# A tuned attention-then-gMLP kernel: more numerator buffers, weights loaded earlier, a shared start, a tail with its own bank waits

## The chip, the cores and the metric

The kernel runs on one core of one Trainium2 chip. The metric is the device time of that core in microseconds (us). Kernels that are compared run on the same chip, in turns with the kernel before. A run over 1.5% above the fastest of its kernel in the same rounds counts as slow.

## The reference, cut to what matters

```python
# q, k, v: (8 batches, 8 heads, 576 rows, 64)
scores = scale * np.matmul(q, k.transpose(0, 1, 3, 2))
thresh = np.max(scores, axis=-1, keepdims=True) - tau
scores = np.where(scores >= thresh, scores, -1000000000.0)
attn = np.exp(scores - max);  attn = attn / (sum + 1e-09)     # shortened
x = (attn @ v) as (batch, 576, 512)                           # shortened
# gMLP:
h = np.maximum(x @ w_in, 0.0);  u, v = halves of h
v_n = normalised v
v_s = np.einsum('ts,bsd->btd', w_spatial, v_n) + b_spatial[None, :, None]
out = (u * v_s) @ w_out
```

## The kernel before

Two heads make a pair, and there are 32 pairs. A pair has four tiles of 128 rows; the 64 rows left over from two pairs make a fifth tile, so there are 144 attention steps. Each step does the following: TensorE multiplies scores into one of two PSUM score buffers (three banks each), DVE takes the row maxima ("negm<-s", 144 of them, the clock of this document), ACT does the exponentials, and DVE zeroes what lies under the threshold (the mask; in some steps ACT does the masking itself, with a steep leaky ReLU ahead of the exponential, and so has one pass more). The numerator, still undivided, is called p. Every second step one DMA transpose turns a numerator buffer into pT (ptr for the left-over rows), which TensorE multiplies with v some steps later. The gMLP of the batch before is woven into the same steps. The last 45 us, after the last score reduction, are gMLP alone; I call them the tail.

The parts that the change and the argument touch:

```python
p_ring = [const.tile([P, 2, 1152], BF16, name=f"p{i}") for i in range(2)]
...
def load_w_in(f):                      # by the software queue, cast on the way; steps 9, 13, 17, 21
    nc.gpsimd.dma_start(out=w_in[:, f, :], in_=moe_w_in[f * P:(f + 1) * P, :])
...
def scores(i, c):                      # c == 4: the left-over rows of two pairs
    s = ps_s.tile([P, 1536], F32, name="s")
    ...
    for n, m, rows in who:             # block-diagonal product: the last 64 keys of both heads
        nc.tensor.matmul(out=view(s[rows], 512, [[448, 2], [1, 64]]), lhsT=qks[n][:, 0, m],
                         rhs=kd_ring[n % 2], start=True, stop=True)
    for h in range(2):                 # the two main products
        hs = slice(64 * h, 64 * h + 64)
        for n, m, rows in who:
            nc.tensor.matmul(out=s[rows, 1024 * h:1024 * h + 512], lhsT=qks[n][hs, 0, m],
                             rhs=qks[n][hs, 1, 0:512], start=True, stop=True)
...
def mask():
    i, c, e = unmasked.pop()
    if c == 4:
        dst = pts[i // 2] = ptr_ring[i // 2 % 2]
        nc.sync.dma_start_transpose(out=dst, in_=pr_ring[i // 2 % 2])
        return
    pt = p_ring[c // 2]
    if not on_act(c):                  # on_act: c in (2, 4)
        ... # DVE: (e >= ctau) * e into pt
    if c % 2:
        dst = pts[i, c // 2] = ptp.tile([P, 2, 9, P], BF16, name="pT")
        nc.sync.dma_start_transpose(...)
...
# after the last step
inner.close()                          # the score buffers' banks go
wide.append(ctx.enter_context(tc.tile_pool(name="ps_t", bufs=6, space=PSUM)))
```

## Time and profile before

| what | before |
|---|---|
| time, median of 3 (range) | 506.18 us (500.98 to 506.64) |
| span of the profiled run | 503.6 us |
| busy: TensorE, DVE, ACT, POOL | 456.3, 415.7, 382.3, 213.0 us |
| mean granted TensorE clock | 0.975 |
| first score reduction starts | 12.30 us |
| reductions of steps 9, 27, 72, 143 start | 34.57, 94.68, 237.58, 458.84 us |

The last two rows cut the span into stretches, by the start of the reduction of step n: the start (to step 0), steps 0-8, 9-26, 27-71, 72-142, and the tail (from the last reduction to the end). In this kernel no average tells the bound, because the stretches have different limits. The views and their lines are in the prediction. Two further lines of busy time by stretch, columns: stretch, its length, busy us (and count) of TensorE, its weight loads, DVE, ACT, POOL, then granted clock, DMA share, GB/s.

```profile
12.30:34.57 22.27, 17.93 (x118) 8.85 (x118) 19.99 (x22) 17.20 (x26) 13.80 (x27) 1.00 0.60 135
34.57:94.68 60.11, 46.32 (x354) 24.60 (x354) 47.23 (x60) 38.94 (x61) 13.48 (x25) 0.83 0.98 176
```

Steps 9 to 26 take 60.1 us, though no engine is busy for more than 47.2 of them.

### The profile page before, as it was taken

What the parts mean: (1) busy time and instruction counts of PE and PEld (TensorE: products, weight loads), DVE (VectorE), ACT (ScalarE), POOL (GpSimd) and SP (SyncE); (2) the same over time, 40 slices, a digit from 0 to 9 for tenths busy, and PEclk for the clock granted to TensorE, in tenths of its full rate; (3) what the DMA queues carried; (4) which work ended last, traced back from release to release, by engine and by line L of the source; (5) the groups of instructions that cost most, each with busy time, mean ns of one, the idle gap of its engine ahead of it and who ended that gap; (6) DMA issues with size and microseconds to landing.
All of it is one profiled execution on the core that took longest, in us unless ns stands there. A gap on an engine that the chain in (4) does not pass through costs nothing.

```text
span 503.6 us, 9909 instructions
## 1 busy us (share of the span) xinstructions
PE 456.3 (91%) x3672; PEld 244.5 (49%) x3672; DVE 415.7 (83%) x559; ACT 382.3 (76%) x665; POOL 213.0 (42%) x408
## 2 busy tenths in 40 slices
PE   7785788988999989989999999999999999997996
PEld 4342444544554535545454545545454545544543
DVE  2896489988979978898889998899879998897463
ACT  2782768888987878877987898887987898885351
POOL 3542122688435634245524644246434643331020
PEclk9997679999999999999999999999999999998999
DMA  7399679997998996989988988999997899667423
GB/s 227 65 238 166 139 160 179 233 219 148 207 176 178 166 219 150 172 193 175 213 209 173 178 199 198 213 170 161 230 209 181 184 198 175 140 117 111 117 67 122
DMA packets 230880, 87.81 MB, mean 174 GB/s; under 512 B 200432, under 2 KB 225520, under 8 KB 230832
## 3 DMA queue, kind: packets, MB, share of 16 engines
q1 hardware_dynamic: 229040, 84.78, 80.8%
q0 software_dynamic: 1376, 2.10, 2.5%
q8 instruction: 29, 0.48, 0.4%
q10 hardware_dynamic: 416, 0.30, 0.2%
q14 instruction: 19, 0.16, 0.1%
HBM read 33.31 MB, written 9.44 MB: 85 GB/s over the span
## 4 chain that ended last, share of the span: by engine, by line
PE 47%; DVE 17%; ACT 14%; DMA 10%; POOL 5%; issue 5%; SPq 1%; ACTq 0%; POOLq 0%
PE s L513 15%; DVE negm L549 8%; DMA pT<-p 6%; DVE p L530 5%; PE s L508 4%; ACT e L570 4%; PE f L482 4%; PE f L224 4%; PE f L257 3%; PE f L423 3%; ACT e L564 2%; PE f L453 2%; ACT vrel L391 1%; DMA uT<-in_moe_w_spatial_dram 1%; PE f L381 1%
## 5 line engine op out<-in xcount | busy, mean ns | idle before, releaser
L549 DVE TENSOR_REDUCE negm<-s 128x2 f32<-128x1152 f32 x144 | 194.8, 1353 | 43.8 <-PE s L513 43.3
L513 PE MATMUL s<-qkT 64*128 64x512 f32 (+1 forms) x640 | 165.4, 650 | 0.0
L530 DVE SCALAR_TENSOR_TENSOR p<-e,ctau 128x1152 bf16<-128x1152 f32 x96 | 138.0, 1438 | 5.0 <-DMA pT<-p 3.0
L570 ACT ACTIVATE e<-s,negm 128x576 f32<-128x576 f32 x192 | 131.9, 742 | 8.8 <-DVE negm L549 7.1
L564 ACT ACTIVATE e<-s,negm 128x576 f32<-128x576 f32 x96 | 66.0, 740 | 31.9 <-DVE negm L553 23.2
L508 PE MATMUL s<-kd,qkT 128*128 128x128 f32 (+1 forms) x320 | 64.1, 305 | 18.4 <-ACT e L570 9.2
L247 POOL COPY kd<-qkT 64x64 f32<-64x64 f32 x64 | 31.0, 484 | 102.1 <-ACT qkT L242 100.3
L508 PEld LDWEIGHTS s<-kd,qkT 128*128 128x128 f32 (+1 forms) x320 | 46.5, 183 | 38.4 <-ACT e L570 15.2
L513 PEld LDWEIGHTS s<-qkT 64*128 64x128 f32 (+1 forms) x640 | 42.6, 177 | 18.7 <-issue 3.6
L257 PEld LDWEIGHTS <-pT 128*128 128x128 bf16 x1024 | 42.3, 98 | 14.3 <-issue 11.3
L257 PE MATMUL f<-v,pT 128*128 128x65 bf16 x992 | 45.4, 195 | 0.0
L566 ACT ACTIVATE p<-e 128x1152 bf16<-128x1152 f32 x32 | 37.2, 1163 | 8.4 <-DMA pT<-p 7.5
L407 POOL TENSOR_SCALAR rs<-ss 128x1 f32<-128x1 f32 (+1 forms) x34 | 7.9, 232 | 72.8 <-ACT sq L405 72.4
L252 PE MATMUL f<-v,pT 128*128 128x130 bf16 x124 | 27.3, 220 | 12.0 <-ACT vrel L391 7.0
L411 POOL TENSOR_SCALAR vn<-vrel,rs,nm 128x512 bf16<-128x512 f32 (+1 forms) x34 | 33.3, 980 | 3.7
L399 POOL TENSOR_SCALAR nmean<-sm 128x1 f32<-128x1 f32 (+1 forms) x35 | 7.7, 220 | 60.4 <-ACT vrel L391 59.9
L453 PE MATMUL f<-wsT,vn 128*128 128x512 bf16 x120 | 29.8, 378 | 2.6 <-ACT qkT L242 2.6
L138 POOL COPY qn<-ql 128x640 f32<-128x640 f32 x32 | 29.7, 929 | 5.5 <-DMA ql<-in_q_dram 3.7
L229 ACT ACTIVATE qkT<-f 128x512 f32<-128x512 f32 x32 | 18.8, 588 | 16.4 <-PE f L224 16.1
L381 PE MATMUL f<-w_in,xT 128*128 128x512 bf16 x112 | 28.8, 380 | 0.0
L423 PE MATMUL f<-xT,w_in 128*128 128x512 bf16 x108 | 27.9, 380 | 0.9 <-DVE xn L266 0.9
L266 DVE TENSOR_TENSOR xn<-f,r 128x256 bf16<-128x256 f32 x62 | 26.3, 425 | 2.1
(156 smaller groups left out, 652.2 us busy)
## 6 DMA issues: line engine op xcount, KB each, us to landing
vl<-in_v_dram SPq DMA_DIRECT2D x16, 512.0 KB, 4.7
ql<-in_q_dram SPq DMA_DIRECT2D x15, 512.0 KB, 4.5
kl<-in_k_dram SPq DMA_DIRECT2D x15, 512.0 KB, 4.5
out_dram<-o SPq DMA_DIRECT2D x20, 256.0 KB, 3.1
uT<-in_moe_w_spatial_dram SPq DMA_DIRECT2D x2, 576.0 KB, 6.2
vl<-in_v_dram SPq DMA_DIRECT2D x16, 64.0 KB, 4.5
pT<-p SPq DMA_TRANSPOSE x64, 5.3
w_in<-in_moe_w_in_dram POOLq DMA_DIRECT2D x4, 256.0 KB, 6.2
```

Source lines behind the costliest of these rows:

```text
L257: nc.tensor.matmul(out=t[:, at + 65 * h:at + 65 * h + 65], lhsT=pt[:, 5 * h + j, :], rhs=vt[:, 6 * h + j, :], start=False, stop=(h == 1 an ...
L381: nc.tensor.matmul(out=t, lhsT=xts[b][:, f, c * P:(c + 1) * P], rhs=w_in[:, f, 512:1024], start=(f == 0), stop=(f == 3))
L411: nc.gpsimd.tensor_scalar(out=dst, in0=vrel[:n], scalar1=rs[:n], scalar2=nm[:n], op0=ALU.mult, op1=ALU.add)
L423: nc.tensor.matmul(out=t, lhsT=w_in[:, m, f * P:(f + 1) * P], rhs=xts[b][:, m, 0:512], start=(m == 0), stop=(m == 3))
L453: nc.tensor.matmul(out=t, lhsT=vn[:, c, f * P:(f + 1) * P], rhs=wsT[:, c, 0:512], start=(c == 0), stop=(c == 4))
L508: nc.tensor.matmul(out=view(s[rows], 512, [[448, 2], [1, 64]]), lhsT=qks[n][:, 0, m], rhs=kd_ring[n % 2], start=True, stop=True)
L513: nc.tensor.matmul(out=s[rows, 1024 * h:1024 * h + 512], lhsT=qks[n][hs, 0, m], rhs=qks[n][hs, 1, 0:512], start=True, stop=True)
L530: nc.vector.scalar_tensor_tensor(out=pt[:, c % 2, :], in0=ef, scalar=ctau, in1=ef, op0=ALU.is_ge, op1=ALU.mult)
L549: nc.vector.tensor_reduce(out=nm, in_=s, axis=AX.X, op=ALU.max, negate=True)
L564: nc.scalar.activation(out=e[:, h, :], in_=s[:, h, :], func=ACT.Prelu, bias=nm[:, h:h + 1], scale=by, alpha=1e30)
L566: nc.scalar.activation(out=pr_ring[i // 2 % 2] if c == 4 else p_ring[c // 2][:, c % 2], in_=e.rearrange("p h s -> p (h s)"), func=ACT.Exp)
L570: nc.scalar.activation(out=e[:, h, :], in_=s[:, h, :], func=ACT.Exp, bias=nm[:, h:h + 1])
```

## The change

Its intent, in parts:

1. **Start.** Fewer warm-up transposes; the first pair is reshaped by DVE, ACT and POOL side by side, transposed into the score buffers and evicted by two engines.
2. **w_in ahead of all steps.** Three of four quarters are loaded by the sync queue before the first step, and POOL casts them. w_out and the bias leave the software queue too; spatial weights are loaded some steps earlier.
3. **Four numerator buffers** instead of two.
4. **The first three left-over tiles (ptr)** are transposed on TensorE instead of by DMA.
5. **Five masks** of the early steps go from DVE to ACT.
6. **Block-diagonal product behind the two main ones**, and the squares of the normalisation come earlier in the code of a step, one step later (`later`).
7. **Tail.** A bank of the score buffers is waited for alone (`reuse_waits="tile"`), and the last chunk of 64 rows becomes two column halves in two banks, stored by two queues.
8. **Small things in the same diff.** The loads of q, k and v go out one per step from step 4 on (before: two per step up to step 10), the order of a step's evictions changes, and the tail takes its banks from the two pools in another rotation.

The diff, cut to its core:

```diff
-    p_ring = [... for i in range(2)]
+    p_ring = [... for i in range(4)]
...
     def load_w_in(f):
-        nc.gpsimd.dma_start(out=w_in[:, f, :], in_=moe_w_in[f * P:(f + 1) * P, :])
+        nc.sync.dma_start(out=wsl[f % 3].rearrange("p c s -> p (c s)")[:, 0:1024],
+                          in_=moe_w_in[f * P:(f + 1) * P, :])
+    def shape_w_in(f):
+        nc.gpsimd.tensor_copy(out=w_in[:, f, :], in_=wsl[f % 3]...[:, 0:1024])
...
+    def first():
+        ts = [ps_s.tile([P, 1536], F32, name="s") for _ in range(2)]
+        ... # nine transposes, evictions by ACT and DVE in turns
...
-            later.append((1, rest))
+            later.append((2, rest))
...
+        for f in due:          # squares: now ahead of the exponentials
+            f()
         e = ep.tile([P, 2, S], F32, name="e")
...
-        return c in (2, 4)
+        return c in (2, 4) or c == 0 and 0 < i < 6
...
-        pt = p_ring[c // 2]
+        pt = p_ring[2 * (i % 2) + c // 2]
...
+    r_on_pe = {0: (9, 11), 1: (18, 20), 2: (25, 27)}
...
-        for _ in range(26):
+        for j in range(3):
+            load_w_in(j)
+        for _ in range(14):
...
-        wide.append(ctx.enter_context(tc.tile_pool(name="ps_t", bufs=6, space=PSUM)))
+        wide.append(ctx.enter_context(tc.tile_pool(name="ps_t", bufs=6, space=PSUM,
+                                                  reuse_waits="tile")))
... # cut: the order of the two products in scores(), the split last chunk, the steps of the weights, part 8
```

## The prediction

> **What bounds the kernel now.** I read the page's forty slices first, then the chain that ended last in order of time, then busy time by stretch, the waits and the DMA queues of the stretches that stood out, and last the times of the 144 score reductions (DVE, "negm<-s"), which mark the 144 attention steps.
>
> The slices: TensorE near full from slice 7 on, but slices 3 to 6 (38 to 75 us) show DVE at 4, a throttled clock, and DMA at nine tenths.
>
> ```profile
> PE   7785788988999989989999999999999999997996
> DVE  2896489988979978898889998899879998897463
> PEclk9997679999999999999999999999999999998999
> DMA  7399679997998996989988988999997899667423
> ```
>
> Busy time by stretch says the same in numbers. Columns: stretch, its length, busy us of PE, its weight loads, DVE, ACT, POOL, then granted clock, DMA share, GB/s.
>
> ```profile
> 14.00:33.00 19.00, 15.02 (x106) 7.22 (x102) 17.10 (x18) 15.48 (x24) 10.59 (x20) 1.00 0.57 116
> 33.00:52.00 19.00, 10.71 (x69) 4.69 (x70) 12.97 (x15) 8.04 (x14) 4.63 (x11) 0.81 1.24 195
> 256.00:312.00 56.00, 53.99 (x448) 28.95 (x446) 49.94 (x64) 47.49 (x84) 26.01 (x49) 1.00 0.90 191
> ```
>
> So there are three regimes. (a) Up to 33 us DVE is fullest (17.1 of 19). (b) From 33 us no engine is full and the DMA share is above 1: transfers bind. (c) In the steady part TensorE is busy 54.0 of 56 us. There, 18 steps take 56.1 us every time (reductions at 237.58, 293.77, 349.85, 405.93).
>
> Regime (b) in the chain (start, length), in the waits of 33 to 57 us, and in the DMA view of the same stretch (packets, MB, share of 16 engines; the last line: us from issue to landing):
>
> ```profile
> 33.29 18.43 DMA pT<-p x2
> ...
> ACT p L566 <- DMA pT<-p: 5.9, 1, 5.9
> PEld L252 <- DMA pT<-p: 5.7, 2, 4.9
> DVE p L530 <- DMA pT<-p: 3.0, 1, 3.0
> ...
> q1 hardware_dynamic: 9493, 3.49, 86.2%
> q0 software_dynamic: 288, 0.52, 17.2%
> ...
> pT<-p SPq DMA_TRANSPOSE x4, 8.0
> ```
>
> DVE and ACT want to overwrite a numerator buffer whose transpose is still under way (two buffers), and TensorE wants its result. Transposes land after 8.0 us here, 5.3 over the whole run. The software queue is the two w_in loads that POOL issues in this stretch. The two queues sum to 103%.
>
> The start (timeline: start, length, engine) and the waits of the tail (458 to 504 us):
>
> ```profile
> 1.35 6.79 PE L737 MATMUL f<-identf 128*128 128x128 f32 x26 [1.35 <-POOL identf masks.py:199]
> 5.02 0.71 POOL L138 COPY qn<-ql 128x640 f32<-128x640 f32 x1 [3.72 <-DMA ql<-in_q_dram]
> 8.12 0.63 PE L224 MATMUL f<-identf,qn 128*128 128x128 f32 x4
> 12.30 1.36 DVE L549 TENSOR_REDUCE negm<-s 128x2 f32<-128x1152 f32 x1 [7.86 <-PE s L513]
> ...
> PE t L366 <- ACT e L570: 2.7, 1, 2.7
> ACT kl L675 <- DVE kl L674: 1.7, 1, 1.7
> ```
>
> Data is there at 5.02, but the 26 warm-up transposes hold TensorE until 8.1, and the first reduction starts at 12.30. In the tail, the first matmul in the new pool waits 2.7 us for the last exponentials, and the last eviction's ACT half waits for its DVE half.
>
> Blocks of nine steps, from the reductions (us): steps 0-8 22.3; 9-17 34.5; 18-26 25.6; 27-35 28.3; 36-44 26.9; 45-53 28.4; 54-62 29.8; 63-71 29.5; steady 28.05 each.
>
> **What the Trainium skill says.** "DMA: Bandwidth & Descriptors", section "Issuing engines are not separate DMA queues": transfers from all issuing engines run on the same 16 DMA engines and interleave. The trace agrees: 86.2% and 17.2%, and transposes 8.0 instead of 5.3 us. The same page, "Latency and other measured facts", puts an effective transpose rate of 261 GB/s. This trace does not agree: in 256 to 312 us the DMA works 0.90 x 56 = 50.4 us. Its loads are 3.5 MB and its stores 1.4 MB, by the list of issues; at 312 GB/s (290 at a share of 0.93 in 10 to 12 us, when only loads ran) they take 15.8 us. That leaves 34.6 us for 5.9 MB of transposes, 171 GB/s, so 3.45 us of all engines for each pT (590 KB) and 1.7 for each ptr. I use these. "TensorE: Matmul & The Clock Gate", "What's actually happening": after an idle window of about 3.4 us the array runs at half clock. The trace agrees: 0.50 from 46 to 58 us, after the stall, and 0.50 in 462 to 464, after the tail's wait. "PSUM — Partial Sum Buffer", "PSUM bank collisions raise a hardware error": no two engines on one bank at once. This fits the 1.7 us wait between two readers of one bank, and the changed tail uses two banks.
>
> **The change, part by part.**
>
> *Start.* Twelve warm-ups fewer: 14 x 0.26 us (6.79/26) end at 5.0 us, as the data lands. The reshaping of q and k goes from POOL in a row (0.71 + 0.61) to DVE, ACT (0.6) and POOL side by side: done at 5.6. Nine transposes at 0.15 (0.63/4) end at 7.0. The evictions are spread, but readers of one bank take turns in the built order, so the last are at about 8.1. Scores take 1.13 + 0.3, so the first reduction is at about 9.5, not 12.30: **-2.8**. The fills that POOL did after the first pair now run while it waits for data: free. On the queue, three w_in loads (1.5 MB) go ahead of the next pairs' q and k. The DMA share is 0.00 from 14 to 20 us, so they use idle time; q and k of pair 2, wanted by TensorE near 21 us, should land by 16.
>
> *Steps 0-8.* DVE loses one mask of 1.41 us, ACT gains one exponential of 1.16. The loop of two score buffers (scores 1.5, reduction 1.36, exponentials 1.38, hand-overs 0.3, over 2) gives 2.3 us per step; now 2.47. **-0.3**.
>
> *Steps 9-26, the main part.* DMA demand before, for nine steps: four pT 13.8, one ptr 1.7, xr 0.2, loads of two pairs 1.76 MB 5.6, and w_in at one per four steps, each 2.1 (17.2% of 24 us, halved), 4.6. Sum 25.9, or 2.9 us per step, before any lost time; observed 60.1/18 = 3.3. After: w_in is gone but for one quarter, the first three ptr are transposed on TensorE (27 transposes of about 0.1 us, 2.7 us in a stretch where it has slack). What remains is 13.8 + 0.2 + 5.6 + about 2.7 (the last quarter of w_in and two spatial weights, in 18 steps) = 22.3, 2.5 per step. With four numerator buffers DVE and ACT no longer wait for the transpose just issued, so a late one is absorbed. Now ACT binds: nine exponential pairs 12.4, five second exponentials 5.8 (of which two are moved from DVE), qkT evictions 2.9, two xT 1.2, two ptr 1.2 = 23.5, or 2.6 per step. DVE is at 22. With 5% slack 2.75 x 18 = 49.5 instead of 60.1: **-10.6**, without the half-clock stretch.
>
> *Steps 27-71.* w_out comes by the sync queue with casts on POOL (0.6 to 0.8 us each, POOL at half load), spatial weights are loaded four steps earlier, so POOL's waits for them (4.9 us, on the chain at 91 to 115 us) shrink. 142.9 us now; TensorE's own busy time in it is 131.9. I take about 40% of the gap: **-4.7**.
>
> *Steady part.* The block-diagonal product (0.31 us net) moves behind the two main products (1.06). Both orders have one change from 64-row to full tiles and one back, so I expect the same TensorE time; weight loads alone could make it +-0.05 us per step. Squares come after the step's other evictions, which frees banks a little sooner. TensorE idles only 2 us in 56. **-1** in all.
>
> *Tail.* Banks freed one by one: the first three belong to the score buffer whose exponentials ended at 458.2, so the 2.7 us wait goes, and with it the half clock afterwards (about 1.5). The last chunk is split in two column halves that can run together (-0.4), its two evictions have a bank each and run side by side (-0.4). **-5**.
>
> Sum: 2.8 + 0.3 + 10.6 + 4.7 + 1 + 5 = 24.4. Span 503.6 - 24.4 = 479.2; the profiled run's time was 505.36 for that span, so add 1.8: **481 us**.
>
> **Rivals.** *DMA still binds early.* For: the three w_in loads and the second pair's loads meet early, and 22.3 us per nine steps leaves little air under ACT's 23.5. Against: the steady part runs at 0.90 without such waits. It would leave steps 9-26 near 55 us: total 487. *ACT becomes the early bound harder than counted*: it was the less loaded engine (15.5 of 19) and gets both exponentials and ptr evictions; at 2.95 per step 485. *The steady part moves*: 117 steps from 27 on, +-0.05 us each, is +-6 us; for a gain: the reduction waits for scores 4.9 us in 56; against: TensorE's work is the same. 475 to 487. *The stall was partly bad luck*: one of three runs of before took 500.98, so the gain against the typical run could be 5 less, but the time after the same.
>
> **Range and chances.** The sure parts (start, tail, the 18 us hole) give about 18 us, already 3.6%. Errors of about 4 us early, 3 in the middle and 4 in the steady part give some 7 together: 472 to 490. Faster by over 2% is below 496: 0.95; within 2%: 0.045; slower: 0.005.
>
> **What would show it.** First reduction near 9.5 us; no DMA wait over 3 us and no clock below 0.9 before 75 us; step 27's reduction near 80 us (now 94.68); step 72's near 218 (now 237.58); steady 56.1 us per 18 steps within 0.5; no wait of TensorE for the last exponentials; from the last reduction to the end 40 us (now 44.8). Wrong if pT transposes still land after 8 us in 30 to 60 us, or if the 18-step period grows.

## The result, and the profile after

The changed kernel took **481.47 us**, the median of 4 runs (480.06 to 483.77); the kernel before took 503.69 in its 4 runs beside them. Ratios in this document are the mean time of one kernel's fast runs over that of the other's fast runs of the same rounds, so not quite the ratio of the medians quoted. Here it is 0.956, with a 95% interval of 0.948 to 0.965. The change is faster by over 2%, and the median lies 0.5 us from the predicted 481.0 (the profiled run, 482.52, lies 1.5 us from it). All outputs are right.

The stretches, from the two profiled runs:

| stretch | before | after | difference | predicted |
|---|---|---|---|---|
| start | 12.30 | 9.64 | -2.7 | -2.8 |
| steps 0-8 | 22.27 | 23.48 | +1.2 | -0.3 |
| steps 9-26 | 60.11 | 49.32 | -10.8 | -10.6 |
| steps 27-71 | 142.90 | 138.61 | -4.3 | -4.7 |
| steps 72-142 | 221.26 | 218.44 | -2.8 | -1 |
| tail | 44.76 | 41.21 | -3.6 | -5 |
| span | 503.6 | 480.7 | -22.9 | -24.4 |

The forty slices of the kernel after:

```profile
PE   7788888889999999899999999999999999999995
DVE  4989888989989997989889888899889998898573
PEclk9899999999999999999999999999999999999999
DMA  7979899979988999998989999987998989677523
```

The hole of DVE and of the clock at slices 3 to 6 of the kernel before is gone. One 8 is left in the clock, at slice 1 (12 to 24 us); it will matter.

Busy time by stretch after (the same columns as before: stretch, length, TensorE, weight loads, DVE, ACT, POOL, clock, DMA share, GB/s), for steps 0-8, steps 9-26 and 18 steady steps:

```profile
9.64:33.12 23.48, 18.80 (x118) 9.17 (x116) 20.12 (x21) 18.52 (x27) 13.12 (x25) 0.93 0.82 219
33.12:82.44 49.32, 41.88 (x377) 23.49 (x378) 43.68 (x59) 45.66 (x71) 18.54 (x30) 1.00 0.96 207
221.05:276.29 55.24, 54.52 (x450) 28.41 (x449) 49.37 (x64) 47.58 (x85) 28.11 (x49) 1.00 0.92 195
```

Nearly the whole gain of steps 9-26 lies in the first nine of them: by the reductions, steps 9-17 went from 34.5 to 23.9 us and steps 18-26 from 25.6 to 25.5. So the change removed one hole; it did not raise the pace of steps 18-26. In steps 9-26 ACT is now the fullest engine, 45.66 of 49.32 us, as the prediction had it (23.5 per nine steps, so 47 in 18). In the steady part the 18-step period went from 56.1 to 55.24 us.

The DMA view (packets, MB, share; us from issue to landing) and the longest waits (us in total, times, longest) in 33 to 57 us, where the prediction showed the transfers of before:

```profile
q1 hardware_dynamic: 12290, 4.74, 93.3%
...
pT<-p SPq DMA_TRANSPOSE x5, 5.9
...
POOL kd L268 <- ACT qkT L263: 14.2, 2, 8.9
PEld s L566 <- issue: 6.9, 9, 0.8
DVE negm L604 <- PE s L566: 2.0, 2, 1.2
```

The software queue is absent here, transposes land after 5.9 us instead of 8.0 (median of 5 and of 4), and no engine's wait for pT is left. Over all of steps 9-26 the median landing is no shorter, 6.1 us after and 5.2 before (9 transposes each): what went is the long ones in the hole. POOL's wait costs nothing: by busy time it has 4.4 us of work in 33 to 52 us.

The start and the end (timeline: start, length, engine, in brackets the idle time before and what ended it):

```profile
2.69 2.55 PE L810 MATMUL f<-identf 128*128 128x128 f32 x9
4.37 0.43 DVE L149 COPY qn<-ql 128x512 f32<-128x512 f32 x1 [0.24 <-DMA ql<-in_q_dram]
4.73 0.62 ACT L149 COPY kn<-kl 128x512 f32<-128x512 f32 x1 [0.51 <-DMA kl<-in_k_dram]
8.05 1.13 PE L563 MATMUL s<-qkT 64*128 64x512 f32 x4 [1.30 <-DVE qkT L283]
9.64 1.36 DVE L604 TENSOR_REDUCE negm<-s 128x2 f32<-128x1152 f32 x1 [1.73 <-PE s L566]
...
439.56 0.40 PE L419 MATMUL t<-w_in,xT 128*64 128x512 bf16 x1
```

Scores start at 8.05 as the last eviction lets them. In the tail the first matmul in the new pool starts 0.07 us after the last reduction does, at 439.49; before it had to wait 2.7 us for the last exponentials.

### The profile page after: what moved, and what is told of

Same layout as the page of the kernel before. It is cut to its first block, busy times and chain, and to the rows that moved or that the text cites. A ratio compares the mean times of both kernels' runs of the same rounds, so it can differ in the third digit from the quotient of the medians.

```text
span 480.7 us, 9934 instructions
## 1 busy us (share of the span) xinstructions
PE 449.2 (93%) x3691; PEld 237.4 (49%) x3691; DVE 410.9 (85%) x563; ACT 390.8 (81%) x677; POOL 226.2 (47%) x403
## 4 chain that ended last, share of the span: by engine, by line
PE 50%; DVE 20%; ACT 19%; issue 7%; DMA 2%; POOL 0%; POOLq 0%; ACTq 0%
PE s L563 16%; DVE negm L604 9%; DVE p L585 7%; PE s L566 6%; ACT e L621 5%; ACT e L627 5%; PE f L294 4%; PE f L476 4%; PE f L245 3%; PE f L506 2%; PE f L535 2%; ACT vrel L444 2%; PE f L289 2%; DMA pT<-p 2%; ACT p L623 1%
## 5 line engine op out<-in xcount | busy, mean ns | idle before, releaser
L585 DVE SCALAR_TENSOR_TENSOR p<-e,ctau 128x1152 bf16<-128x1152 f32 x91 | 132.9, 1461 | 1.2 <-ACT e L627 1.1
L566 PEld LDWEIGHTS s<-kd,qkT 128*128 128x128 f32 (+1 forms) x320 | 41.5, 178 | 110.7 <-issue 100.1
L268 POOL COPY kd<-qkT 64x64 f32<-64x64 f32 x62 | 27.0, 435 | 101.3 <-ACT qkT L263 99.5
L566 PE MATMUL s<-kd,qkT 128*128 128x128 f32 (+1 forms) x320 | 69.9, 322 | 0.0
L452 POOL TENSOR_SCALAR nmean<-sm 128x1 f32<-128x1 f32 (+1 forms) x35 | 16.5, 472 | 68.1 <-ACT vrel L444 63.0
L623 ACT ACTIVATE p<-e 128x1152 bf16<-128x1152 f32 x37 | 43.0, 1163 | 1.2
L136 POOL COPY qn<-ql 128x640 f32<-128x640 f32 x31 | 35.0, 1129 | 15.0 <-DMA ql<-in_k_dram 11.0
L464 POOL TENSOR_SCALAR vn<-vrel,rs,nm 128x512 bf16<-128x512 f32 (+1 forms) x34 | 29.6, 872 | 3.7
L252 ACT COPY qkT<-f 128x512 f32<-128x512 f32 x31 | 18.2, 588 | 12.8 <-PE f L245 12.8
L156 POOL CAST v<-vl 128x640 bf16<-128x640 f32 x32 | 26.4, 824 | 1.6 <-DMA vl<-in_v_dram 1.6
```

The source lines that it names most:

```text
L136: nc.gpsimd.tensor_copy(out=t, in_=ld_ring[i // 2 % 2][w][:, 2 * (i % 2):2 * (i % 2) + 2].rearrange("p h c d -> p c h d"))
L585: nc.vector.scalar_tensor_tensor(out=pt[:, c % 2, :], in0=ef, scalar=ctau, in1=ef, op0=ALU.is_ge, op1=ALU.mult)
L623: nc.scalar.activation(out=pr_ring[i // 2 % 2] if c == 4 else p_ring[2 * (i % 2) + c // 2][:, c % 2], in_=e.rearrange("p h s -> p (h s)"), ...
```

## The experiments

Twelve kernels ran, in four calls, each call on one chip: first the four that follow the kernel after in the table; then x_rest_by_dma, x_masks_on_dve, x_block_first and z_pair2_first; then x_squares_old, x_pool_waits and x_last_chunk_old; then w_combined. The kernel before ran in each call; the kernel after did not. There are two kinds: "x_", "z_" and "w_" start from the changed kernel and undo or alter a part; "y_" start from the kernel before and do one part alone. The rival theories were that one part made the whole gain, that the parts add up, or that some of them are redundant or harmful. The stretches of all profiled runs (us):

| kernel | start | 0-8 | 9-26 | 27-71 | 72-142 | tail | span |
|---|---|---|---|---|---|---|---|
| before | 12.30 | 22.27 | 60.11 | 142.90 | 221.26 | 44.76 | 503.6 |
| after | 9.64 | 23.48 | 49.32 | 138.61 | 218.44 | 41.21 | 480.7 |
| y_w_in_ahead | 12.21 | 22.62 | 51.30 | 144.05 | 222.44 | 43.08 | 495.7 |
| y_four_buffers | 11.53 | 25.35 | 54.40 | 143.27 | 221.09 | 44.96 | 500.6 |
| x_w_in_software | 9.76 | 22.22 | 49.84 | 137.09 | 218.47 | 41.02 | 478.4 |
| x_two_buffers | 9.36 | 23.81 | 50.70 | 138.94 | 224.01 | 41.28 | 488.1 |
| x_rest_by_dma | 9.77 | 22.58 | 47.59 | 137.48 | 218.51 | 40.97 | 476.9 |
| x_masks_on_dve | 9.24 | 24.91 | 50.84 | 137.31 | 219.21 | 41.29 | 482.8 |
| x_block_first | 9.55 | 22.59 | 48.98 | 138.29 | 218.31 | 41.28 | 479.0 |
| z_pair2_first | 9.68 | 23.41 | 49.37 | 137.04 | 219.08 | 41.22 | 479.8 |
| x_squares_old | 9.18 | 23.31 | 49.06 | 138.20 | 221.12 | 41.23 | 482.1 |
| x_pool_waits | 9.48 | 23.36 | 49.21 | 137.04 | 219.12 | 43.69 | 481.9 |
| x_last_chunk_old | 9.76 | 22.52 | 49.08 | 137.02 | 219.31 | 40.91 | 478.6 |
| w_combined | 9.24 | 22.43 | 48.30 | 139.98 | 218.50 | 40.75 | 479.2 |

Each row is one execution, so I read a difference only where it is larger than what unrelated runs show. In steps 27-71 eight undone kernels lie between 137.0 and 138.3, and the kernel after has one late transpose that costs it some 1.6 us there; differences below that are not read. In 72-142 the runs that leave that part alone spread from 218.4 to 219.3.

### w_in by the software queue again (x_w_in_software), and w_in ahead alone (y_w_in_ahead)

```diff
 # x_w_in_software, from the kernel after
-        nc.sync.dma_start(out=wsl[f % 3]..., in_=moe_w_in[f * P:(f + 1) * P, :])
+        nc.gpsimd.dma_start(out=w_in[:, f, :], in_=moe_w_in[f * P:(f + 1) * P, :])
-    chores[13] = (load_w_in, 3)
-    for gs_, f in (((4, 5, 6, 17), shape_w_in),
+    for gs_, f in (((9, 13, 17, 21), load_w_in),
-        for j in range(3):
-            load_w_in(j)
 # y_w_in_ahead, from the kernel before: the same in the other direction
```

Expected of x_w_in_software:

> The changed kernel, but with w_in loaded again in four parts by POOL's software queue with the cast, at steps 9, 13, 17 and 21. Theory (the first weights' load was what oversubscribed the DMA engines early): the stretch of steps 9 to 26 grows from 49.3 us to 53 or more, transposes in it land after 7 us or more instead of 5.9, and the whole is 484 to 490 us. Rival (four buffers absorb late transposes whatever the load): steps 9 to 26 stay within 1 us of 49.3, and the time within 1.5 us of 481.5, or below it, because steps 0 to 8 lose the wait for pair 2 and become 22 instead of 23.5 us.

Expected of y_w_in_ahead:

> The kernel before, with only this changed: w_in by the sync queue ahead of all steps, cast by POOL at steps 4, 5, 6 and 17. Theory: the DMA hole after 39 us closes, steps 9 to 26 fall from 60.1 us to 50 to 53, the clock stays at 0.95 or more there, total 492 to 497 us. Rival (buffers): steps 9 to 26 stay at 56 or more, total 499 or more.

Measured: x_w_in_software 480.69 us (479.67 to 481.48), ratio to before 0.956 [0.950, 0.963]: the same as the kernel after. y_w_in_ahead 498.81 (496.40 to 501.98), ratio 0.9926 [0.9856, 0.9995]. In its profile steps 9-26 took 8.8 us less than in the one profiled run of before; the medians of these rounds differ by only 3.8 (before: 502.61), so the hole in that profiled run was one of the deeper ones, or the stretches give some of it back: both kernels vary. The stretch did as the theory of y_w_in_ahead said (50 to 53 us), the total missed its 492 to 497. For x_w_in_software the theory fell and the rival held.

In x_w_in_software, busy time by stretch of steps 9-26 and the software queue in it (packets, MB, share):

```profile
31.98:81.82 49.84, 41.95 (x381) 23.70 (x380) 42.94 (x60) 45.80 (x71) 17.37 (x33) 1.00 1.08 202
...
q0 software_dynamic: 576, 1.05, 14.1%
```

The DMA share is 1.08, higher than in the kernel before (0.98), and the stretch still takes only 49.84 us. So the early load of w_in closes most of the profiled hole in the old kernel, but it is not needed in the new one. DMA demand alone, which my working took for the bound, does not explain the 60 us.

A share of 1 is also not the ceiling that my working took it for. It sums the time of packets, and these overlap on an engine. In the kernel before, only transposes ran in 298 to 300.5 us (every packet under 512 B; packets, MB, share):

```profile
q1 hardware_dynamic: 2148, 0.54, 115.6%
```

So the engines moved 217 GB/s at a share of 1.16, and with almost only other transfers in 302.5 to 303.5 us 387 GB/s at 1.09. At these rates the work that the prediction sums to 25.9 us per nine steps takes about 21.6 (an estimate: a pT 2.7, a ptr 1.4, two pairs' loads 4.5, w_in and xr as there), or 43 us of the 60. The two kernels are not quite equal in DMA work, though: share times length gives 58.9 us of packet time before and 53.8 here, where the two ptr of the stretch are on TensorE and one spatial weight more is loaded.

### Two buffers again (x_two_buffers), and four buffers alone (y_four_buffers)

```diff
-    p_ring = [... for i in range(4)]
+    p_ring = [... for i in range(2)]
-        pt = p_ring[2 * (i % 2) + c // 2]
+        pt = p_ring[c // 2]
 # y_four_buffers, from the kernel before: the same in the other direction
```

Expected of x_two_buffers:

> The changed kernel, but with two numerator buffers instead of four. Theory (w_in's move is the larger part, the buffers only absorb): steps 9 to 26 take 49.3 to 51.5 us, DVE and ACT together wait under 3 us for the transposes there, total 481.5 to 484. Rival (the two buffers were the bottleneck): steps 9 to 26 take 54 us or more, total 486 or more, and the steady period of 18 steps goes from 55.2 back towards 56.1 us.

Expected of y_four_buffers:

> The kernel before, with only this changed: four numerator buffers. Theory: the DMA engines have the same work, so TensorE still waits for late transposes; steps 9 to 26 take 55 to 60 us, total 498 to 503. Rival: they fall to 52 or less, total 495 or less.

Measured: x_two_buffers 489.28 (487.66 to 490.70), ratio 0.973 [0.967, 0.979]; y_four_buffers 504.30 (501.45 to 506.41), ratio 1.003 [0.996, 1.010]. All four kernels of these two sections ran on one chip, so the two undone kernels can be set against each other: two buffers cost 8.6 us against x_w_in_software. For x_two_buffers the rival held for the whole (486 or more) and for the period, the theory for steps 9-26; y_four_buffers fell between its two, with 54.40 us and no gain in total.

The waits for transposes over the whole run of x_two_buffers, and over steps 9-26 of y_four_buffers:

```profile
ACT p L623 <- DMA pT<-p: 8.5, 9, 1.6
...
PEld L252 <- DMA pT<-p: 6.8, 4, 3.4
PE f L252 <- DMA pT<-p: 4.3, 3, 2.5
```

With two buffers it is ACT that waits to overwrite one; with four, only TensorE waits, for the result. So the mechanism (a buffer still under transpose) is real, but it is worth only 1.4 us in steps 9-26 of the new kernel, and nothing in steps 9-17, where the old hole was (23.9 us with two buffers and with four). Most of the loss, 5.6 us, is in steps 72-142, where I had counted no gain from buffers: the period is 56.1 to 57.9 us instead of 55.24, and 5.0 of ACT's 8.5 us of waits lie in 221 to 447 us. In the old kernel four buffers change nothing there (period 56.06). Buffers and the new order of a step (the squares, below) work together: neither gives the 55.24 alone. Two buffers and the software queue for w_in together, in the new kernel, were not run; that would show whether the old hole comes back when both of its remedies go.

That the start of the steps of y_four_buffers is slow (25.35 us for 0-8) goes with a clock of 0.64 in 20 to 26 us; it hides part of what the four buffers gain afterwards.

### The left-over tiles by DMA again (x_rest_by_dma), the masks on DVE again (x_masks_on_dve)

```diff
 # x_rest_by_dma
-    r_on_pe = {0: (9, 11), 1: (18, 20), 2: (25, 27)}
+    r_on_pe = {}
 # x_masks_on_dve
-        return c in (2, 4) or c == 0 and 0 < i < 6
+        return c in (2, 4)
```

Expected of x_rest_by_dma:

> The changed kernel, but the first three remainder blocks (ptr) are transposed by the DMA queue again instead of TensorE. The software w_in run showed that 7.5 us more DMA work in steps 9 to 26 costs only 0.5 us there. Theory now (the moved transfers each matter little by themselves once nothing else holds the loop): these 2 x 1.7 us cost under 1 us in steps 9 to 26 (49.3 now), or gain up to 2 us, because ACT loses four copies of 0.6 us; total 479 to 483. Rival (the ptr move is what kept the software run from the hole): steps 9 to 26 grow to 52 or more, total 484 or more.

Expected of x_masks_on_dve:

> The changed kernel, but the first row block's masks of pairs 1 to 5 stay on DVE. Theory of the prediction (ACT binds early in the changed kernel at 2.6 us per step and DVE would be at 24 to 25 us per nine steps without the move): steps 9 to 26 stay within 49 to 52, total 481 to 484. Rival (moving work from DVE to ACT is the main gain of the early part): steps 9 to 26 at 54 or more, total 486 or more.

Measured: x_rest_by_dma 479.06 (478.67 to 481.17), ratio 0.950 [0.946, 0.955]; x_masks_on_dve 483.03 (481.56 to 484.58), ratio 0.956 [0.951, 0.962]. These two share a chip with x_block_first (480.42) and z_pair2_first (480.98). Both theories held.

Steps 9-26 of x_rest_by_dma:

```profile
32.35:79.94 47.59, 39.94 (x354) 22.18 (x356) 43.03 (x59) 42.64 (x65) 17.35 (x29) 1.00 1.04 213
```

ACT loses 3.0 us of evictions (45.66 to 42.64) and the stretch loses 1.7, at a higher DMA share. So part 4 of the change cost time (1.0 us by w_combined, which has the same edit): it takes work off the DMA, which does not bind here, and gives it to ACT, the fullest engine. TensorE loses 1.9 us too (41.88 to 39.94), so that it is ACT's part that counts is read from the busy times and not shown alone. The masks are the opposite case. Steps 9-26 of x_masks_on_dve:

```profile
34.15:84.99 50.84, 41.54 (x376) 23.43 (x378) 49.45 (x60) 41.86 (x67) 19.84 (x30) 1.00 1.00 203
```

With the masks on DVE the stretch is 1.5 us longer, and DVE the fullest engine. The rest of what this kernel loses to its chip-mates is in steps 0-8 (24.91 us, with a clock of 0.51 in 20 to 26 us), which is the next section's matter. ACT and DVE are near each other in this stretch, and which of them has the moved work shows.

### Pair 2 ahead of w_in (z_pair2_first)

TensorE at half clock in 20 to 26 us made steps 0-8 slower than predicted. My theory was that POOL waits for pair 2's q and k behind the w_in loads (5.2 us in 9 to 34 us) and so holds TensorE.

```diff
+        for w in (0, 1):
+            for f in load(2, 2, w):
+                f()
         for j in range(3):
             load_w_in(j)
 # cut: these loads are left out of the queue of step 0
```

> The changed kernel, with q and k of pairs 2 and 3 issued ahead of the three w_in loads instead of behind them. In the changed kernel POOL waits 5.2 us for them (they take 9 us to land) and steps 0 to 8 take 23.5 us; without w_in in front they took 22.2. Theory: steps 0 to 8 become 22.0 to 22.5, and about 1.2 us of the whole is gained, 480.3 in the median, span 479 to 480. Rival: the w_in casts at steps 4 to 6 now wait and hold POOL, steps 0 to 8 stay at 23 or more, no gain.

Measured: 480.98 (480.31 to 482.24), ratio 0.954 [0.950, 0.957]. POOL's wait went from 5.2 to 0.5 us, but steps 0-8 still took 23.41 us, with a clock of 0.72 in 20 to 26 us. The theory falls: the wait was real and hidden.

What does separate the runs is the clock itself. In 20 to 26 us it is 0.73 in the kernel after, and 0.51 to 0.93 in the five others built from it that took 23.3 us or more for steps 0-8; it is 1.00 in x_w_in_software, x_rest_by_dma, x_block_first and x_last_chunk_old, which took 22.2 to 22.6. The last of them does not differ from the kernel after in anything before the tail, and neither does x_pool_waits, at 0.76. The same matmuls (timeline) in the kernel after, and then in x_last_chunk_old:

```profile
19.75 2.04 PE L563 MATMUL s<-qkT 64*128 64x512 f32 x4 [1.13 <-ACT e L627]
```

```profile
19.88 1.13 PE L563 MATMUL s<-qkT 64*128 64x512 f32 x4 [1.13 <-ACT e L627]
```

The idle time before is the same, 1.13 us, and the matmuls take 2.04 us in one and 1.13 in the other. So with the same code before it this lightly loaded stretch is throttled in one execution and not in another, which I call chance, and it is worth about 1 us of 23.

### The order of the products (x_block_first), and the place of the squares (x_squares_old)

```diff
 # x_block_first: the loop of the block-diagonal product moved ahead of the main products again
 # x_squares_old
-            later.append((2, rest))
+            later.append((1, rest))
-        for f in due:            # ahead of the exponentials
-            f()
         ...
         unmasked.append((i, c, e))
+        for f in due:
+            f()
```

Expected of x_block_first:

> The changed kernel, with the block-diagonal product ahead of the two main products again. Theory (the steady gain of 0.95 us per 18 steps comes from this order: scores start without waiting for POOL's kd and the next full-array weights load under the block product): the 18-step period goes from 55.24 to 55.8 to 56.3, total 484 to 487. Rival (it comes from the squares' new place or the buffers): the period stays within 0.2 of 55.24, total 481 to 482.5.

Expected of x_squares_old:

> The changed kernel, with the squares of the normalization back at their old place, after a step's exponentials instead of ahead of the next step's. Theory (the score order makes the steady gain): the 18-step period stays within 0.3 of 55.24, total 481 to 483. Rival (this place makes it, by freeing banks earlier): the period goes to 55.8 or more, total 484 or more.

Measured: x_block_first 480.42 (479.00 to 481.52), ratio 0.952 [0.947, 0.957], period 55.20 us. x_squares_old 484.22 (483.80 to 487.28), ratio 0.962 [0.956, 0.967], period 55.66 to 56.18 and 72-142 at 221.12, almost the 221.26 of before. On the chip of x_squares_old, x_last_chunk_old took 480.85 us. In both runs the theory fell and the rival held.

POOL's waits for the squares in 18 steady steps (us in total, times, longest), in x_squares_old and in the kernel after:

```profile
POOL rs L460 <- ACT sq L458: 11.0, 5, 4.0
```

```profile
POOL rs L460 <- ACT sq L458: 2.5, 4, 0.9
```

So the order of the products is worth nothing, and the squares' place is worth 1.8 us (against x_last_chunk_old) to 2.7 us (against the kernel after) over steps 72-142. POOL now waits far less for ACT's squares; but it has 28 us of work in 55 and is not the bound, so this is a sign of the move and not the path of the gain. By which release the period shortens was not isolated.

### The tail: waits for the whole pool (x_pool_waits), and the last chunk in one piece (x_last_chunk_old)

```diff
 # x_pool_waits
-        wide.append(... bufs=6, space=PSUM, reuse_waits="tile")))
+        wide.append(... bufs=6, space=PSUM)))
 # x_last_chunk_old: five banks; one 512-column product of 64 rows; DVE copies one half, then ACT the
 # other; one store by the sync queue
```

Expected of x_pool_waits:

> The changed kernel, with the tail's pool of banks waiting as a whole again. Theory: TensorE waits 2.5 to 3 us for the last exponentials and then runs at half clock, the first tail matmul moves from 0.07 us after the last reduction to 2.8 us after it, and the time from the last reduction to the end grows from 41.2 to 44.5 to 45.5, total 485. Rival (the tail's transposes by DMA bind anyway): it grows by under 1.5 us, total 483 or less.

Expected of x_last_chunk_old:

> The changed kernel, with the last 64 rows as one product of 512 columns, its two evictions from one bank one after the other, and one store on the sync queue. In the changed kernel the store phase after the last matmul is 0.7 us longer than in the kernel before. Theory (two small stores on two queues, landing after 3.2 us instead of 2.3, give back what the split saves): time from the last reduction to the end stays within 0.4 us of 41.2, total 481 to 482. Rival (the split is worth its 0.8 us): it grows to 41.8 or more.

Measured: x_pool_waits 483.56 (483.17 to 483.70), ratio 0.958 [0.953, 0.963], tail 43.69 us; x_last_chunk_old 480.85 (479.42 to 481.65), ratio 0.953 [0.949, 0.956], tail 40.91 us. The wait is back in x_pool_waits (from its waits in the tail):

```profile
PE t L419 <- ACT e L627: 2.7, 1, 2.7
```

It makes the tail 2.5 us longer, so nearly all of it lay on the path. The half clock that the theory expected after it did not come, so the tail missed the 44.5 to 45.5 us. The half clock that followed it in the kernel before is a matter apart. The first 7 us of the tail by busy time (columns as above), in the kernel before, and in y_w_in_ahead, whose tail has the same code and the same wait of 2.7 us:

```profile
458.84:466.00 7.16, 4.49 (x38) 2.52 (x35) 4.05 (x8) 3.97 (x8) 0.18 (x1) 0.76 0.71 132
```

```profile
452.60:460.00 7.40, 4.68 (x47) 2.69 (x46) 4.06 (x8) 5.33 (x10) 0.18 (x1) 1.00 0.72 134
```

In about the same time TensorE got through 38 matmuls in the one and 47 in the other, and the tails are 44.76 and 43.08 us. The clock is 0.77 in y_four_buffers (tail 44.96) and 1.00 in x_pool_waits. So the half clock costs about 1.1 to 1.7 us where it falls, and after the same wait it falls in some runs only. With the wait gone the clock was 1.00 in these first 7 us in every profile.

The split chunk gains nothing and loses about 0.3 us (the theory for x_last_chunk_old). The stores at the very end (KB each, us to landing), in the kernel after and in x_last_chunk_old:

```profile
out_dram<-kl SPq DMA_DIRECT2D x1, 64.0 KB, 3.3
out_dram<-vl ACTq DMA_DIRECT2D x1, 64.0 KB, 3.2
```

```profile
out_dram<-kl SPq DMA_DIRECT2D x1, 128.0 KB, 2.4
```

By the timelines, the stores of the split form are issued 1.05 and 1.33 us after the chunk's first matmul (474.97; 476.02 and 476.30), the single one 1.93 us after it (473.17; 475.10). So the split gains 0.6 to 0.9 us on the engines, close to the 0.8 that I had counted, and its two half-size stores then take 0.8 to 0.9 us longer. From that matmul to the end it is 5.7 us with the split and 5.4 without.

### Combined (w_combined)

The kernel after, with the last chunk in one piece, the left-over tiles by DMA, and four identity transposes more in each of steps 1 to 6, meant to keep TensorE's clock up.

```diff
-    r_on_pe = {0: (9, 11), 1: (18, 20), 2: (25, 27)}
+    r_on_pe = {}
+            if 1 <= g <= 6:
+                fs.append(("act", keep_warm, lambda: None))   # four transposes of identf into bank()
 # and x_last_chunk_old's edit
```

> Three things the runs pointed to, each in its own stretch of the changed kernel: all ptr blocks by the DMA queue (steps 9 to 26 were 47.6 us so, against 49.0 to 49.4 in the seven runs with them on TensorE and four buffers), the last 64 rows as one product (tail 40.9 instead of 41.2), and four extra transposes of a constant on TensorE in each of steps 1 to 6, in its idle time. Theory for the last: steps 0 to 8 took 22.5 us in every profile where the clock stayed at 1.00 from 20 to 26 us and 23.3 or more where it fell to 0.51 to 0.76, and POOL's wait for pair 2 had no part in it; with the filling the clock stays at 1.00 and steps 0 to 8 take 22.2 to 22.6. Together: span 475.5 to 477.5, median 477.5 to 479.5. Rival (the filling delays the evictions that ACT waits for, or the clock falls all the same): steps 0 to 8 at 23 or more.

Measured: 480.38 (477.87 to 483.85), ratio 0.949 [0.944, 0.954]. The median missed the expected 477.5 to 479.5. The clock stayed at 1.00 in 20 to 26 us and steps 0-8 took 22.43 us, as expected; but since the clock did so in four kernels without the filling, this one profile does not show that the filling did it. Steps 9-26 took 48.30, the tail 40.75. A late transpose cost it some 2.5 us in 27-71, with a clock of 0.94 there. It beats the kernel before clearly. Its interval and that of x_rest_by_dma (0.950 [0.946, 0.955]) overlap that of the kernel after (0.956 [0.948, 0.965]), so neither is shown to be faster than the change as it was made.

## Why the prediction was right or wrong

**The time was right** (481.47 against 481.0, inside 472 to 490), and three of the six terms (the start, steps 9-26, steps 27-71) came within 0.4 us. The others were off by 1.5 to 1.8 us, two for the worse and one for the better. That the total came within 0.5 us is partly luck, and not every term came for the reason given.

- *Start: right.* -2.7 us against -2.8 by the trace (no run takes it back); the first reduction is at 9.64 ("about 9.5").
- *Steps 0-8: the term failed.* "-0.3" was worked out from the loop of two score buffers at full clock. The runs at full clock give 22.2 to 22.6 us, so about +0.2 instead of -0.3; the kernel after adds 1 us of half clock. I knew the throttle from two stalls, but did not ask which other stretch was light enough for it.
- *Steps 9-26: the size was right, its working only half so.* That late transposes held the engines in 33 to 57 us, and that ACT would be the fullest engine afterwards, both show (transposes 8.0 to 5.9 us; ACT 45.66 of 49.32 us). What failed is the sum of DMA demand as the whole explanation, in three ways. It counts packet time, whose share passes 1 when the engines are merely full (1.16 for transposes alone), so 25.9 us per nine steps is some 21.6 of real time. It is a pace, but the loss was one hole: 25.9 fits steps 18-26 (25.6 us, before and after alike) and leaves 8.6 of the 34.5 us of steps 9-17 unexplained. And with w_in back on the software queue and a DMA share of 1.08 the new kernel needs 49.84 us. In the old kernel w_in ahead alone gives -8.8, four buffers alone -5.7, and undoing either in the new one costs +0.5 and +1.4. The remedies overlap; they do not add up. And "the first three ptr are transposed on TensorE" was a loss of 1.7 us in this term. Why the old kernel with four buffers still needs 54.40 us at a DMA share of 1.03, where the new one needs 49.84 at 1.08, is not settled: it has the masks on DVE (47.0 us busy), a clock of 0.94, two ptr on the DMA, its spatial weights later, and its loads sent two per step up to step 10; no run alters this last alone. Part of the 10.8 us is the throttle that followed the hole: TensorE was busy 46.32 us for 354 matmuls at a clock of 0.83, and 41.91 us for 353 in y_w_in_ahead at 0.97.
- *Steps 27-71: about right.* -4.3 against -4.7; the eight undone kernels that lie between 137.0 and 138.3 have -4.6 to -5.9. POOL's 4.9 us of waits for spatial weights are gone from this stretch, as foreseen, but one of 4.6 us now lies before 75 us; the 40% taken of the gap was a guess that held (of 11.8 us: TensorE's busy time there is 131.1, not 131.9). No run takes the weights' new path back, so its part in this is not shown.
- *Steady part: mis-sized.* "-1" measured -2.8. The squares' new place I had named as a cause; the buffers I had counted for steps 9-26 only, and that is the step that failed. Each of the two alone decides the whole: without the squares' move 221.12, with two buffers 224.01, against 218.44. That I expected no change from the order of the products was right (55.20 against 55.24). My check, "56.1 us per 18 steps within 0.5", failed at 55.24, on the good side.
- *Tail: mis-sized.* "-5" measured -3.6. The wait gave 2.5 where 2.7 stood. Of the 44.76 - 43.69 = 1.1 us that remain, the split chunk took 0.3, so the half clock gave about 1.4 where 1.5 stood (1.7 by y_w_in_ahead), with the new rotation of banks in the same sum. The term that failed is the split chunk: 0.3 us of loss where 0.4 + 0.4 of gain stood, because the gain on the engines went into slower stores. And where the prediction sees an idle window of 3.4 us behind the half clock of 462 to 464 us, TensorE had idled 2.67 us only (458.98 to 461.65), and after the same wait y_w_in_ahead was not throttled: the agreement holds for the stall (idle for 3.63 us, to 45.94), not for the tail.

Of the checks: "no DMA wait over 3 us before 75 us" holds for TensorE, DVE and ACT, but not for POOL, which waited 5.2 us for pair 2 and 4.6 us for spatial weights; step 27's reduction came at 82.44 ("near 80"), step 72's at 221.05 ("near 218"), the tail at 41.2 ("40"). "No clock below 0.9 before 75 us" failed, in 20 to 26 us.

Of the rivals, *DMA still binds early* fell (49.3, not 55 us). *ACT becomes the early bound harder than counted* did not come true (49.3 us is 2.74 per step, not 2.95), though the ptr evictions moved onto ACT came with a loss. *The steady part moves* came true for the better. *Partly bad luck* holds in part: over all rounds the fast runs of the kernel before ranged from 500.20 to 509.39 us, the kernel after, in its four runs, from 480.06 to 483.77; how deep the hole was in each of those runs the profiles cannot say.

## What to carry to other kernels

When a stall has several causes that meet (a late transfer, too few buffers, a throttled clock), each remedy alone can remove much of it (here 8.8 and 5.7 of 10.8 us, in one profile each); cost them one at a time from both ends, by doing one alone and undoing one, before crediting any, and take out those that load the engine that binds next. A sum of work against a resource shows that it can bind, not that it does: nearly the same transfers at a higher share did no harm in the changed kernel. Measure first what share the resource shows when it is full, and look whether the loss is a pace or one hole. At the end of a kernel nothing hides a store, so a cut that starts it earlier and makes it smaller has to be measured from the first matmul to the end.

## What the Trainium skill lacked or had wrong

- "TensorE: Matmul & The Clock Gate", "A second HAM failure mode: psum-queue depth-cycling", says that frequent short idles can throttle the array again. The runs agree: with idle gaps of 1.1 to 1.3 us the clock in 20 to 26 us was 0.73 in one run and 1.00 in another of the same early code (2.04 against 1.13 us for four matmuls). What it lacks is how much work suffices. The runs do not settle it either: the clock was 1.00 with TensorE busy 5.28 of 6 us (w_combined, with four transposes more per step), but also with 4.08 of 6 us (x_last_chunk_old).
- "DMA: Bandwidth & Descriptors", "Latency and other measured facts": the transpose rate of 261 GB/s does not hold here. Where only transposes ran, the trace has 217 GB/s (kernel before, 298 to 300.5 us). The prediction's 171 GB/s divides by packet time, which overlaps, and is too low as a rate.
- No page that I read has what halving a last store costs: two stores of 64 KB in rows of 1 KB, on two queues at once, landed after 3.2 to 3.3 us, one of 128 KB in rows of 2 KB after 2.3 to 2.4. Which of size, rows and queues does it was not tried.
- "Perfetto Trace Analysis", "Identifying the Most-Contended Engine", has no figure for the busy share that the 16 DMA engines show when they are full. By the sum of packet times it is over 1 here: 1.16 with transposes alone (217 GB/s), 1.09 with almost only other transfers (387 GB/s). So 18 steps could take 49.84 us at 1.08 in the changed kernel.
